# A token-mixing transformer block on one core: another order of scores, projections and sums in the last cycle of attention, from score tile 998 on

## The chip, the core and the metric

The kernel runs on one core of one Trainium2 chip. Its time is the device time of one launch in microseconds (us); the time of a version is the median of a few runs. The engines named here are PE (TensorE, with PEld for its weight loads), ACT (ScalarE), DVE (VectorE), POOL (GpSimd) and SP, which issues the DMAs. Each engine works through its own queue in order and waits on semaphores for the others.

## What is computed

Two layers, each of them multi-query attention (32 query heads, one key and value head) and a token-mixing MLP, over a sequence of 2048 tokens of width 512. Both parts start with a layer norm and add to the residual. Cut to what matters:

```python
def _A_ref(x, wq, wk, wv, wo):            # S = 2048, D = 512, H = 32, Dh = 16
    q = (x @ wq).reshape(B, S, H, Dh).transpose(0, 2, 1, 3)
    k = x @ wk
    v = x @ wv
    scores = jnp.einsum("bhqd,bkd->bhqk", q, k) * (Dh ** -0.5)
    p = softmax(scores, axis=-1)
    o = jnp.einsum("bhqk,bkd->bhqd", p, v)
    return o.transpose(0, 2, 1, 3).reshape(B, S, H * Dh) @ wo

def _B_ref(x, w1, b1, w2, b2):            # F = 1792
    h = _layernorm(x)
    u = gelu(jnp.einsum("bsd,sf->bdf", h, w1) + b1)
    y = jnp.einsum("bdf,fs->bds", u, w2) + b2
    return y.transpose(0, 2, 1)

for _ in range(2):
    x = x + _A_ref(_layernorm(x), A_wq, A_wk, A_wv, A_wo)
    x = x + _B_ref(_layernorm(x), B_w1, B_b1, B_w2, B_b2)
```

## The kernel before

**Attention in tiles.** A layer's attention is cut into 32 groups: group i has four heads and one block of 512 queries. A group has 32 score tiles: 16 key tiles of 128 keys (kt) times two pairs of heads (j0 = 0 or 2). So a layer has 1024 tiles, and tile 998 is group 31 (the last), kt = 3, j0 = 0. A tile's name below is sc_31_3_0, its exponentials are p_31_3_0, and its sums go into acc_31. Tile 998 is reached once in each layer.

A tile passes three steps:

- `scores` (line 921): two matmuls of 51 rows put the scores of two heads into a PSUM pair `sc`. There are three such pairs (`bufs=3`), so a score waits until the tile three before it has left its pair.
- line 931: ACT takes the exponential from the pair into an SBUF tile `p`. For a **copied** tile DVE first copies the pair to SBUF (line 929), which frees the pair, and ACT works on the copy in place.
- `sums` (line 937): matmuls of 32 columns add p times the values (and a column of ones, the softmax's denominator) into `acc`.

There are 12 buffers for p: eight of one pool (`NP`) and, from the third guard on, every third tile uses one of four others (`NMORE`).

**Other work between the tiles.** When two groups (eight heads) are done, DVE divides by the denominators (lines 857 to 863) and writes `hl`. A projection (line 898) multiplies 128 tokens of it by a part of `wo` into a PSUM bank `po`; DVE adds the bank to the residual `x` (line 906). The projections of one turn use the same bank, so one waits for the addition of the one before. At tile 998 four projections po_14_0 to po_14_3 of one part, three matmuls each, are due. The MLP's own products (line 1214) run after attention has ended, in `rest`, beginning with pu_e.

**What sets the order.** `Attention.run` writes every engine's queue by hand, by tuples of numbers ("turns"). A number from 1 to 9 stands for that many scores; 11 to 19 for as many as its last digit, the last of them copied; 0 for the next of the other parts (here a projection); -n for the sums of the n oldest tiles that wait. At each negative number there is also a slot in which small DVE work may be put (`mix.step`). `Mixer.turn` chooses the tuple: FOURS is taken where four projections are due, 30 tiles of the last group are still to be summed, and more than 992 tiles are scored. It is taken at tile 998, once in each layer. The turns behind it are PLAIN, two scores and then as many sums as leave two tiles waiting:

```python
PLAIN = (2, -2)
...
if len(self.projections) > 3 and att.to_boundary() == 30 and att.scored > 2 * NKT * (NB * NG - 1):
    return FOURS, [projection] * 4
```

Of the kernel before, what the change touches and what calls it, by code (L numbers as in the profile page):

```python
# [45 lines left out]
    2, -2, 13, 0, 13, -4, 13, 0, 13, -4, 3, -6, 13, 0, 13, 0, 3, -6, 13, -4, 3, -4,  # L46
)
ENTRY = (1, 0, 13, 0, 13, -4, 13, -4, 13, -4, 13, -4)
FOURS = (3, -4, 12, 0, 13, 0, -4, 3, -4, 12, 0, 13, -4, 0)
SHORT = (2, 0, 3, -4, 3, -4)  # L50
TINY = (2, 0, 2, -4)
PLAIN = (2, -2)
# [20 lines left out]
def kernel(  # L73
# [729 lines left out]
    class Attention:  # L803
# [193 lines left out]
        def run(self, mix, proj):  # L997
# [10 lines left out]
            while self.scored < total:  # L1008
# [31 lines left out]
                for k in turn:  # L1040
# [15 lines left out]
                    else:  # L1056
# [11 lines left out]
                        if self.pieces:  # L1068
                            self.pieces.pop(0)()
                        elif turn in (LONG, COPIED, ENTRY, DOUBLE, QUAD, QUAD_TO_FOUR, FOURS, WHOLE):  # L1070
                            room = 2.4 if turn in (COPIED, ENTRY, QUAD, QUAD_TO_FOUR) else 1.0
# [15 lines left out]
    class Mixer:  # L1087
# [150 lines left out]
        def turn(self, att):  # L1238
# [20 lines left out]
            if len(self.projections) > 3 and att.to_boundary() == 30 and att.scored > 2 * NKT * (NB * NG - 1):  # L1259
                return FOURS, [projection] * 4  # L1260
            if len(self.projections) > 1:
# [473 lines left out]
```

## Time and profile before

| | us |
|---|---|
| runs (3), median | 2511.52 |
| runs, lowest to highest | 2510.51 to 2512.19 |
| the profiled execution: its own time | 2511.45 |
| the profiled execution: span from first to last instruction | 2509.7 |
| busy in the span: PE, ACT, DVE, POOL | 2493.1, 2102.5, 1554.8, 148.2 |
| FOURS and the turns behind it, layer 0: first score, first product behind attention | 1013.14, 1041.00 |

A timeline's row has a start, a duration (both us), the engine, the line, the operation with what it writes and reads, and how many instructions are merged in it; in brackets stands the idle time before it and what ended that. A score tile is two matmuls, so "sc x6" is three tiles; the sums of a tile are four, so "acc x16" are the sums of four tiles. PE's durations overlap those behind them, so what a piece costs on PE is the distance from its start to the next piece's start.

### The profile page before, as it was taken

How to read it: one execution, taken by the hardware profiler on the slowest of the kernel's cores; microseconds unless marked ns; L12 is line 12 of the kernel's file. 1: busy time of each engine (PE TensorE's matmuls, PEld its weight loads, DVE VectorE, ACT ScalarE, POOL GpSimd, SP SyncE). 2: the span in 40 equal slices, each digit the busy share in tenths (PEclk: the TensorE clock that was granted, in tenths of full speed). 3: DMA queues.
4: the chain of work that ended last, by engine and by line, in shares of the span. 5: the costliest groups of instructions: out<-in, count | busy, mean ns of one | idle time of the engine just before them, and what ended most of it. 6: DMA issues, size and time to landing. Idle time of an engine off the chain costs nothing. (4 is left out here: it accounts for less than half of the span.)

```text
span 2509.7 us, 41974 instructions
## 1 busy us (share of the span) xinstructions
PE 2493.1 (99%) x16170; PEld 1242.5 (50%) x16170; DVE 1554.8 (62%) x2462; ACT 2102.5 (84%) x2345; POOL 148.2 (6%) x235
## 2 busy tenths in 40 slices
PE   9999999999999999999999999999999999999999
PEld 6444344444444444588864343444444444445887
DVE  6565566667766776564445565666677667765522
ACT  6999999999999999653349999999999999995511
POOL 5000000000000000141000000000000000002200
PEclk9999999999999999999999999999999999999999
DMA  3221201111111111134414112111111111102343
GB/s 116 75 66 41 65 29 39 32 41 31 39 31 39 31 41 31 43 110 149 127 51 126 51 47 57 31 39 31 41 31 39 31 43 33 41 26 67 106 125 95
DMA packets 168679, 143.56 MB, mean 57 GB/s; under 512 B 17650, under 2 KB 132368, under 8 KB 167952
## 3 DMA queue, kind: packets, MB, share of 16 engines
q1 hardware_dynamic: 168464, 140.72, 18.9%
q8 instruction: 132, 2.16, 0.4%
q14 instruction: 83, 0.68, 0.1%
HBM read 97.67 MB, written 26.22 MB: 49 GB/s over the span
## 5 line engine op out<-in xcount | busy, mean ns | idle before, releaser
L931 ACT ACTIVATE p<-sc 128x1024 f32<-128x1024 f32 x1441 | 1404.4, 1050 | 63.5 <-PE sc L921 62.7
L929 DVE COPY p<-sc 128x1024 f32<-128x1024 f32 x607 | 742.7, 1224 | 525.2 <-PE sc L921 439.6
L937 PE MATMUL acc<-p,vaug 128*32 128x512 f32 x8192 | 999.7, 600 | 0.0
L921 PE MATMUL sc<-qs,kst 51*128 51x512 f32 x4096 | 683.4, 432 | 8.2 <-DVE kst L595 2.7
L931 ACT ACTIVATE p<-p 128x1024 f32<-128x1024 f32 x607 | 659.4, 1086 | 12.9 <-DVE p L929 8.2
L921 PEld LDWEIGHTS sc<-qs,kst 51*128 51x128 f32 x4096 | 338.8, 185 | 560.1 <-ACT p L931 390.2
L937 PEld LDWEIGHTS acc<-p,vaug 128*32 128x32 f32 x8192 | 218.6, 109 | 488.9 <-issue 474.6
L1467 PE MATMUL py<-u,w 128*128 128x512 f32 x1344 | 307.4, 390 | 0.0
L1467 PEld LDWEIGHTS py<-u,w 128*128 128x128 f32 x1344 | 251.9, 188 | 52.3
L1455 ACT CAST w<-w2r 128x896 fp32r<-128x896 f32 x64 | 60.3, 945 | 185.6 <-PE py L1467 177.8
L1214 PE MATMUL pu<-hb,w 128*128 128x512 f32 x792 | 209.6, 406 | 0.0
L1214 PEld LDWEIGHTS pu<-hb,w 128*128 128x128 f32 x792 | 140.9, 188 | 57.7 <-issue 31.8
L1201 POOL TENSOR_TENSOR w<-w1r,w 128x256 fp32r<-128x256 f32 x86 | 69.9, 821 | 1572.9 <-ACT w L1199 1571.8
L1456 DVE TENSOR_TENSOR w<-w2r,w 128x896 fp32r<-128x896 f32 x64 | 72.3, 1130 | 110.7 <-ACT w L1455 110.7
L857 DVE RECIPROCAL o<-o 128x128 f32<-128x128 f32 x120 | 113.3, 944 | 8.8 <-DMA o<-ev 8.8
L898 PE MATMUL po<-wo,hl 128*128 128x512 f32 x360 | 100.5, 412 | 0.1
L418 PE MATMUL pq<-hT,wq 128*128 128x512 f32 x312 | 81.4, 404 | 0.0
L898 PEld LDWEIGHTS po<-wo,hl 128*128 128x128 f32 x360 | 62.6, 188 | 34.0 <-issue 16.4
L839 DVE COPY ev<-acc 128x512 f32<-128x512 f32 x64 | 43.6, 682 | 56.0 <-PE acc L937 56.0
L1214 PE MATMUL pu_l<-hb,w 128*128 128x512 f32 x336 | 77.1, 389 | 0.0
L1473 DVE SCALAR_TENSOR_TENSOR x<-py,b2c,x 128x512 f32<-128x512 f32 x32 | 24.0, 750 | 81.6 <-PE py L1467 81.6
L1199 ACT CAST w<-w1r 128x256 fp32r<-128x256 f32 x86 | 34.3, 406 | 47.3 <-PE pu_l L1214 12.7
(191 smaller groups left out, 1181.9 us busy)
## 6 DMA issues: line engine op xcount, KB each, us to landing
w1r<-in_B_w_dram SPq DMA_DIRECT2D x224, 128.0 KB
w2r<-in_B_w_dram SPq DMA_DIRECT2D x64, 448.0 KB
qs<-qd SPq DMA_DIRECT2D x384, 64.0 KB
qd<-q SPq DMA_DIRECT2D x64, 256.0 KB
o<-ev SPq DMA_DIRECT2D x128, 128.0 KB
x<-in_A_x_dram SPq DMA_DIRECT2D x16, 256.0 KB
hd<-hT SPq DMA_DIRECT2D x2, 2048.0 KB
out_dram<-x SPq DMA_DIRECT2D x16, 256.0 KB
```

What stands on the lines that cost most here:

```text
L418: yield nc.tensor.matmul(out, a, c, start=(k == 0), stop=(k == len(terms) - 1))
L857: nc.vector.reciprocal(o[:, 1, c], o[:, 1, c])
L898: nc.tensor.matmul(po, a, c, start=(k == 0), stop=(k == 3 * len(parts) - 1))
L921: nc.tensor.matmul(sc[:, j, :], kst[kt // 4][rows, kt % 4 * P : (kt % 4 + 1) * P], qs[i % NQ][rows, j0 // 2, :], start=True, stop=True,)
L929: nc.vector.tensor_copy(pt, sc)
L931: nc.scalar.activation(pt, sc, AF.Exp, scale=0.25)
L937: nc.tensor.matmul(self.acc[i][c : c + 32, :], vaug[:, kt].rearrange("p d k -> p (d k)"), pt[:, j, :], start=(kt == 0), stop=(kt == NKT - ...
L1201: eng.tensor_tensor(w[:, 1], raw, f32(w[:, 0]), op=ALU.subtract)
L1214: nc.tensor.matmul(pu, a, c, start=(start and k == 0), stop=(stop and k == 5))
L1455: nc.scalar.copy(w[:, 0], raw)
L1456: nc.vector.tensor_tensor(w[:, 1], raw, f32(w[:, 0]), op=ALU.subtract)
L1467: nc.tensor.matmul(py, a, d, start=(c == 0 and f == 0 and k == 0), stop=(c == 1 and f == NFH - 1 and k == 2),)
```

## The change

One tuple has other numbers. Both have 16 scores, 16 sums, four projections and four slots; one more score is copied by DVE in the new one.

```diff
 ENTRY = (1, 0, 13, 0, 13, -4, 13, -4, 13, -4, 13, -4)
-FOURS = (3, -4, 12, 0, 13, 0, -4, 3, -4, 12, 0, 13, -4, 0)
+FOURS = (-2, 13, 0, 13, 0, 13, 0, -2, -6, 13, 0, 13, -6, 1)
 SHORT = (2, 0, 3, -4, 3, -4)
```

PE's queue at tile 998 of layer 0, before:

```order
L921 MATMUL sc_31_3_0_10975<-qs_90,kst_84 128x512 x2
L921 MATMUL sc_31_3_2_10980<-qs_90,kst_84 128x512 x2
L921 MATMUL sc_31_4_0_10985<-qs_90,kst_85 128x512 x2
L937 MATMUL acc_31_10967<-p_31_1_0_10925,vaug 32x512 x2
L937 MATMUL acc_31_10967<-p_31_1_2_10945,vaug 32x512 x2
L937 MATMUL acc_31_10967<-p_31_2_0_10950,vaug 32x512 x2
L937 MATMUL acc_31_10967<-p_31_2_2_10955,vaug 32x512 x2
L921 MATMUL sc_31_4_2_10998<-qs_90,kst_85 128x512 x2
L921 MATMUL sc_31_5_0_11003<-qs_90,kst_85 128x512 x2
L898 MATMUL po_14_0_11009<-wo_1151,hl_14_10757 128x512 x3
L921 MATMUL sc_31_5_2_11014<-qs_90,kst_85 128x512 x2
```

The same place with the change:

```order
L937 MATMUL acc_31_10967<-p_31_1_0_10925,vaug 32x512 x2
L937 MATMUL acc_31_10967<-p_31_1_2_10945,vaug 32x512 x2
L921 MATMUL sc_31_3_0_10979<-qs_90,kst_84 128x512 x2
L921 MATMUL sc_31_3_2_10984<-qs_90,kst_84 128x512 x2
L921 MATMUL sc_31_4_0_10989<-qs_90,kst_85 128x512 x2
L898 MATMUL po_14_0_10995<-wo_1151,hl_14_10757 128x512 x3
L921 MATMUL sc_31_4_2_11000<-qs_90,kst_85 128x512 x2
L921 MATMUL sc_31_5_0_11005<-qs_90,kst_85 128x512 x2
L921 MATMUL sc_31_5_2_11010<-qs_90,kst_85 128x512 x2
L898 MATMUL po_14_1_11016<-wo_1151,hl_14_10757 128x512 x3
```

Two tiles' sums stand ahead of tile 998 now, and blocks of three scores and a projection follow each other without sums between them; a third such block (6_0, 6_2, 7_0 and po_14_2) follows.

PE's queue behind that third block, before (where po_14_2 stands later, behind 9_0):

```order
L921 MATMUL sc_31_7_0_11043<-qs_90,kst_85 128x512 x2
L921 MATMUL sc_31_7_2_11048<-qs_90,kst_85 128x512 x2
L921 MATMUL sc_31_8_0_11053<-qs_90,kst_86 128x512 x2
L937 MATMUL acc_31_10967<-p_31_5_0_11006,vaug 32x512 x2
L937 MATMUL acc_31_10967<-p_31_5_2_11017,vaug 32x512 x2
L937 MATMUL acc_31_10967<-p_31_6_0_11022,vaug 32x512 x2
L937 MATMUL acc_31_10967<-p_31_6_2_11027,vaug 32x512 x2
L921 MATMUL sc_31_8_2_11066<-qs_90,kst_86 128x512 x2
```

And with the change:

```order
L921 MATMUL sc_31_7_0_11031<-qs_90,kst_85 128x512 x2
L898 MATMUL po_14_2_11037<-wo_1151,hl_14_10757 128x512 x3
L937 MATMUL acc_31_10967<-p_31_2_0_10950,vaug 32x512 x2
L937 MATMUL acc_31_10967<-p_31_2_2_10955,vaug 32x512 x2
L937 MATMUL acc_31_10967<-p_31_3_0_10982,vaug 32x512 x2
L937 MATMUL acc_31_10967<-p_31_3_2_10987,vaug 32x512 x2
L937 MATMUL acc_31_10967<-p_31_4_0_10992,vaug 32x512 x2
L937 MATMUL acc_31_10967<-p_31_4_2_11003,vaug 32x512 x2
L937 MATMUL acc_31_10967<-p_31_5_0_11008,vaug 32x512 x2
L937 MATMUL acc_31_10967<-p_31_5_2_11013,vaug 32x512 x2
L921 MATMUL sc_31_7_2_11058<-qs_90,kst_85 128x512 x2
```

Eight tiles' sums stand in one run between the scores of 7_0 and 7_2, where four stood between blocks of three before. Further on, 8_0, 8_2, po_14_3, 9_0, 9_2 and 10_0 follow, then six sums in one run, then 10_2 and the PLAIN turns as before: 11_0, 11_2, the sums of 9_0 to 10_2, and 12_0.

DVE's queue in the same stretch, with the change:

```order
L863 TENSOR_TENSOR hl_14_10757<-o_28_10380,hl_14_10757 128x128
L929 COPY p_31_4_0_10992<-sc_31_4_0_10989 128x1024
L906 TENSOR_TENSOR x_80<-x_80,po_14_0_10995 128x512
L929 COPY p_31_5_2_11013<-sc_31_5_2_11010 128x1024
L906 TENSOR_TENSOR x_81<-x_81,po_14_1_11016 128x512
L929 COPY p_31_7_0_11034<-sc_31_7_0_11031 128x1024
L906 TENSOR_TENSOR x_82<-x_82,po_14_2_11037 128x512
L929 COPY p_31_8_2_11071<-sc_31_8_2_11068 128x1024
L906 TENSOR_TENSOR x_83<-x_83,po_14_3_11074 128x512
L929 COPY p_31_10_0_11092<-sc_31_10_0_11089 128x1024
```

Before, the copies stood at 5_0, 6_2, 9_0 and 10_2, each ahead of one of the four additions, and there was no fifth. The queues of POOL and SP keep their order. Layer 1 is changed in the same way.

## The prediction, on record before the changed kernel was run

> **What bounds the kernel now.** I read the page first, then the chain of waits, then ACT and PE row by row around the first of the two places that change.
>
> ```profile
> PE 2493.1 (99%) x16170; PEld 1242.5 (50%) x16170; DVE 1554.8 (62%) x2462; ACT 2102.5 (84%) x2345; POOL 148.2 (6%) x235
> ```
>
> By this line PE is never idle, but a PE row also contains the time in which a matmul that has been issued waits for data. So I look at the chain that ended last, at the end of layer 1's attention (start, length, what):
>
> ```profile
> 2276.47 1.85 PE acc L937 x16
> 2278.33 0.67 PE sc L921 x4
> 2278.99 1.00 PE acc L937 x8
> 2279.99 0.66 PE sc L921 x4
> 2280.65 1.26 PE acc L937 x8
> ...
> 2284.40 3.00 PE acc L937 x16
> 2287.40 2.99 PE pu_e L1214 x12
> ```
>
> The same four tiles' sums cost 1.85 us at the top and 3.00 at the bottom. The difference is waiting for exponentials, and it ends in the first product of the MLP. So what delays ACT's last exponential delays all that follows. ACT's rows in layer 0, from tile 3_0 (at 1013.97) on, those at which its spacing changes:
>
> ```profile
> 1013.97 1.04 ACT L931 ACTIVATE p<-sc 128x1024 f32<-128x1024 f32 x1
> 1016.68 1.07 ACT L931 ACTIVATE p<-sc 128x1024 f32<-128x1024 f32 x1
> 1017.99 1.06 ACT L931 ACTIVATE p<-p 128x1024 f32<-128x1024 f32 x1 [0.23 <-DVE p L929]
> 1018.95 1.01 ACT L931 ACTIVATE p<-sc 128x1024 f32<-128x1024 f32 x1
> 1020.76 1.06 ACT L931 ACTIVATE p<-p 128x1024 f32<-128x1024 f32 x1
> 1021.95 1.02 ACT L931 ACTIVATE p<-sc 128x1024 f32<-128x1024 f32 x1
> 1024.70 1.03 ACT L931 ACTIVATE p<-sc 128x1024 f32<-128x1024 f32 x1
> 1026.20 1.06 ACT L931 ACTIVATE p<-p 128x1024 f32<-128x1024 f32 x1 [0.47 <-DVE p L929]
> 1030.94 1.01 ACT L931 ACTIVATE p<-sc 128x1024 f32<-128x1024 f32 x1
> 1032.53 1.02 ACT L931 ACTIVATE p<-sc 128x1024 f32<-128x1024 f32 x1 [0.58 <-PE sc L921]
> 1038.88 1.09 ACT L931 ACTIVATE p<-sc 128x1024 f32<-128x1024 f32 x1
> ```
>
> Unhindered, an exponential from PSUM takes 0.905 from start to start (1013.97 to 1016.68 is three of them), and a copied one 0.955 (1017.99 to 1018.95). From 12_0 (1032.53) to 15_2 (1038.88), seven steps take 6.35, so there ACT is the bound and whatever moves 12_0 moves the end by as much. From 3_0 to 12_0 there are 18 steps in 18.56 us; 14 x 0.905 + 4 x 0.955 is 16.49, so ACT **starves for 2.07 us** per layer. That is the quantity on which the change acts. PE's rows beside it, with the prices of its pieces (start to next start):
>
> ```profile
> 974.37 2.78 PE L937 MATMUL acc<-p,vaug 128*32 128x512 f32 x24
> 977.08 0.97 PE L921 MATMUL sc<-qs,kst 51*128 51x512 f32 x6
> ...
> 1013.14 0.96 PE L921 MATMUL sc<-qs,kst 51*128 51x512 f32 x6
> 1013.48 0.62 PE L921 MATMUL sc<-qs,kst 51*128 51x512 f32 x4
> 1014.03 1.92 PE L937 MATMUL acc<-p,vaug 128*32 128x512 f32 x16
> 1015.88 0.73 PE L921 MATMUL sc<-qs,kst 51*128 51x512 f32 x4
> 1016.55 0.97 PE L898 MATMUL po<-wo,hl 128*128 128x512 f32 x3
> 1017.45 1.10 PE L921 MATMUL sc<-qs,kst 51*128 51x512 f32 x6
> ...
> 1021.35 0.97 PE L921 MATMUL sc<-qs,kst 51*128 51x512 f32 x6
> 1031.93 0.73 PE L921 MATMUL sc<-qs,kst 51*128 51x512 f32 x4
> 1032.59 1.07 PE L937 MATMUL acc<-p,vaug 128*32 128x512 f32 x8
> 1033.59 0.73 PE L921 MATMUL sc<-qs,kst 51*128 51x512 f32 x4
> ```
>
> Three scores cost 0.89, of which 0.55 from the second's start; two cost 0.67; a projection costs 0.90. Sums cost 1.00 for two tiles, 1.85 for four, 2.71 for six, so 0.86 for each pair more. Three scores take 0.89 on PE and 2.72 to 2.77 on ACT, so PE fills the three PSUM pairs and then waits for ACT, as it does once already:
>
> ```profile
> 1017.81 0.38 PEld L921 LDWEIGHTS sc<-qs,kst 51*128 51x128 f32 x4 [0.18 <-ACT p L931]
> ```
>
> This is the weight load of 6_0, held until the exponential of 4_2 (the 1016.68 row), three tiles before, had left its pair: 1.13 after that began; in a row of exponentials they last 1.02, so I take **1.10** (between 1.07 and 1.13). And a starved ACT begins **0.60** after the score's start: 1021.35 to 1021.95, and 1031.93 to 1032.53.
>
> **The change, step by step, in one layer.** PE reaches the stretch at 1013.14, ACT is free for 3_0 at 1013.97. Nothing ahead of it has moved. I follow where ACT starves in the new order.
>
> *The two tiles' sums first.* 1013.14 + 1.00 for the sums + 0.60 is 1014.74, when 3_0 can begin: ACT waits **0.77** where it waited for nothing.
>
> *The three projections three tiles apart.* Here ACT is fed from full pairs and sets the pace. Let E be the start of 5_0's exponential. 6_2 takes over 5_0's pair at E + 1.10; from there 7_0 and its handing over cost 0.55, po_14_2 0.90, and the run of eight sums 3.57 (2.71 + 0.86, an estimate from the rows, since no run of eight is shown here). So 7_2's score begins at E + 6.12 and can be taken up at E + 6.72. Meanwhile ACT has 5_0, 5_2 (copied), 6_0, 6_2 and 7_0 (copied): 3 x 0.905 + 2 x 0.955 = 4.63. ACT waits **2.09**.
>
> *The six sums.* With E the start of 8_0's: 9_2 at E + 1.10, then 0.55, six sums 2.71 and 0.60 make E + 4.96, against the same 4.63. ACT waits **0.33**.
>
> *The end.* From 10_2's score, three scores (0.89) and four sums (1.85) make 2.74 until 12_0's, against three exponentials, 2.72: **0.02**.
>
> Together 3.21 instead of 2.07, and one more copied tile costs ACT 0.05: **1.19 us per layer**, twice **2.4 us**. From 12_0 on the queues are the old ones and ACT is the bound as before, so nothing of it is given back.
>
> What is covered: DVE's work per block is one copy and one addition.
>
> ```profile
> 1013.78 0.29 DVE L863 TENSOR_TENSOR hl<-o,hl 128x128 fp32r<-128x128 f32 x1
> 1016.73 1.22 DVE L929 COPY p<-sc 128x1024 f32<-128x1024 f32 x1 [2.65 <-PE sc L921]
> 1017.87 0.68 DVE L906 TENSOR_TENSOR x<-x,po 128x512 f32<-128x512 f32 x1
> ```
>
> That is 1.14 + 0.68 = 1.82 us in a block of 2.77 on ACT, so the fifth copy, and the wait of one projection for the addition of the one before, lie beside ACT's work. The cover is 0.95 per block; beyond it each microsecond on DVE would delay the block by as much. `hl` is ready at 1014.07, and the first projection comes after the sums and three scores, 1013.14 + 1.00 + 0.89 = 1015.03. Up to eleven tiles wait for their sums (from 2_0 to 7_0); there are 12 buffers, and 7_0 takes that of 1_0, summed at the start, so no buffer is waited for. No DMA is issued in the stretch on either side, the division of tile 14's part is done, and the four slots find nothing to place, so SP, POOL and the rest of DVE are not touched.
>
> The second place is the same; its rows stand 16.64 apart as here 1015.88 and 1032.53 do (16.65):
>
> ```profile
> 2262.22 0.73 PE L921 MATMUL sc<-qs,kst 51*128 51x512 f32 x4
> 2278.86 7.44 ACT L931 ACTIVATE p<-sc 128x1024 f32<-128x1024 f32 x8 [0.58 <-PE sc L921]
> ```
>
> The profiled execution took 2511.45 (span 2509.7) and the median is 2511.52, 0.07 apart, so the sum is put on the median: **2513.9**. The bounds: 3.44 to 3.70 for the eight sums (eight at the 0.43 of a pair's half; twice 1.85), 1.07 to 1.13 for a pair's release twice. They leave 1.0 to 1.4 per layer; with the runs' own spread of 0.8 to each side the case lies between 2512.7 and 2515.1.
>
> **The rivals.** *PE's work alone counts.* The page's 99% and a chain that is PE nearly throughout speak for it. Until 12_0's score PE had blocks of 3, 2, 3, 3, 2, 3 and 2 scores, 4 x 0.89 + 3 x 0.67 = 5.57, and five runs of sums, 9.25; now it has six blocks of three, 5.34, and runs of 2, 8, 6 and 4, 1.00 + 3.57 + 2.71 + 1.85 = 9.13. That is 0.35 less per layer, so 2510.8. It decides if the pairs come free early enough that no score waits. Against it: the 1017.81 row waits already after a single block, and the stretch took 18.79 for 18.42 of work; the forecast needs 1.9 us of waiting in it. Chance 0.12. The Trainium skill's page "TensorEngine Tiling (Array Packing)", Key Properties, says that changing the tiling mode drains TensorE; scores, sums and projections use three shapes, and the new order changes shape less often, so by that rule the change ends at this rival's time. The rows above agree that a change of shape costs something (two sums 1.00, but 0.86 for two more).
>
> *The clock drops, and it ends slower.* In the blocks of projections PE waits for some 0.4 to 0.6 us before several scores, some 1.3 us in three. If that lowered the granted clock to half for the run of eight sums, they would cost 3.57 more per layer: 2513.9 + 7.1 = 2521.0. It decides from the point where waiting of this density is punished. Against it stands the end of attention, where the sums wait likewise:
>
> ```profile
> 1034.20:1041.00 6.80, 6.80 (x42) 1.75 (x40) 0.00 (x0) 6.05 (x8) 0.67 (x1) 1.00 0.00 0
> ```
>
> The granted clock there (third from the end) is 1.00. Chance 0.04. The Trainium skill's page "TensorE: Matmul & The Clock Gate", section "A second HAM failure mode: psum-queue depth-cycling", says that small idle pieces at PSUM's hand-over can make the clock swing between half and full; that rule would give this rival's time, and the row just shown disagrees with it so far.
>
> *ACT no longer starves.* More tiles are scored ahead, and if those covered the long runs of sums, 2.07 per layer would go: 2507.4. It decides if more than 3.57 + 0.90 + 0.60 us of exponentials were ready as PE turns to the eight sums. But a score needs a pair, and only a copied tile waits outside, so there are at most three. Chance 0.03. *The branch isn't taken* and nothing changes, 2511.5: both engines' queues show the new order, so 0.01.
>
> **How the numbers follow.** The forecast has 0.80, the rivals 0.12, 0.04, 0.03 and 0.01. The range takes in the first rival and the forecast's bounds, with some tenths beyond each for what a launch varies: 2510.6 to 2515.8. A measurement of this kernel tells about 0.2% (5 us) from no change. The forecast (0.1%) and the first, third and last rival lie within; slower by more are the clock and a forecast mis-sized by a factor of two, 0.06; faster by more is nearly excluded, since even an ACT that never starves gains 0.16%: 0.02.
>
> **What would show it.** In the changed profile, ACT should wait about 0.8 before 3_0, 2.1 before 7_2 and 0.3 before 10_2, and not between 4_0 and 7_0; weight loads of scores should wait for ACT in the first three blocks; from 12_0 to pu_e all should be as long as before, and pu_e begin 1.2 later at layer 0 and 2.4 at layer 1. I am wrong if 7_2's exponential follows 7_0's closely (more tiles were ready than I count), if a projection waits for DVE's addition after PE's other waits are over, or if the granted clock falls below 1.00 in the stretch.

## The result, and the profile after

| | before | with the change |
|---|---|---|
| runs, median (22 each), us | 2512.10 | 2515.47 |
| runs, lowest to highest, us | 2509.75 to 2513.86 | 2513.13 to 2517.85 |
| span of the profiled execution, us | 2509.7 | 2512.0 |

The ratio is 1.0013, with a 95% interval from 1.0007 to 1.0019: the change costs 3.4 us, between 1.8 and 4.8. The time moved the way that was forecast. It lies in the range, above the forecast of 2513.9 by 1.6; of these, 0.6 come from the base, whose median was 2511.52 over three runs and is 2512.10 over 22. The prediction had said that a measurement of this kernel tells about 0.2% from no change; 22 runs of each kernel told 0.13%. One of the 15 runs of the kernel before that were taken beside the experiments needed 8570.69 us at a mean granted clock of 0.265, and the interval given below leaves it out.

The page's totals hardly move, and that is the first thing to see: the line that said nothing before says nothing now.

```profile
PE 2492.3 (99%) x16170; PEld 1242.6 (49%) x16170; DVE 1556.4 (62%) x2464; ACT 2102.4 (84%) x2345; POOL 147.9 (6%) x235
```

The change shows in ACT's timeline in layer 0 (start, duration, operation, number merged, idle time and what ended it), from the tile ahead of 998 on:

```profile
1012.08 1.08 ACT L931 ACTIVATE p<-p 128x1024 f32<-128x1024 f32 x1
1013.66 1.94 ACT L931 ACTIVATE p<-sc 128x1024 f32<-128x1024 f32 x2 [0.51 <-PE sc L921]
1015.48 1.06 ACT L931 ACTIVATE p<-p 128x1024 f32<-128x1024 f32 x1
1016.43 1.94 ACT L931 ACTIVATE p<-sc 128x1024 f32<-128x1024 f32 x2
1018.24 1.08 ACT L931 ACTIVATE p<-p 128x1024 f32<-128x1024 f32 x1
1019.19 1.96 ACT L931 ACTIVATE p<-sc 128x1024 f32<-128x1024 f32 x2
1021.00 1.09 ACT L931 ACTIVATE p<-p 128x1024 f32<-128x1024 f32 x1
1024.15 1.94 ACT L931 ACTIVATE p<-sc 128x1024 f32<-128x1024 f32 x2 [2.07 <-PE sc L921]
1025.98 1.06 ACT L931 ACTIVATE p<-p 128x1024 f32<-128x1024 f32 x1
1026.93 1.94 ACT L931 ACTIVATE p<-sc 128x1024 f32<-128x1024 f32 x2
1028.74 1.08 ACT L931 ACTIVATE p<-p 128x1024 f32<-128x1024 f32 x1
1030.13 10.19 ACT L931 ACTIVATE p<-sc 128x1024 f32<-128x1024 f32 x11 [0.32 <-PE sc L921]
```

The first row is 2_2, then come 3_0 (1013.66), 7_2 (1024.15) and 10_2 (1030.13). Before each of these three ACT is idle and PE's scores end the wait; from 3_0 to 7_0 and from 7_2 to 10_0 it is fed without a gap, and the last eleven run in one piece. Counted from start to start, with 0.905 or 0.955 for the tile ahead, it waits 0.62, 2.19 and 0.43 there. PE's timeline shows the other side:

```profile
1010.34 2.78 PE L937 MATMUL acc<-p,vaug 128*32 128x512 f32 x24
1013.06 0.97 PE L921 MATMUL sc<-qs,kst 51*128 51x512 f32 x6
1013.95 0.96 PE L898 MATMUL po<-wo,hl 128*128 128x512 f32 x3
1014.85 0.51 PE L921 MATMUL sc<-qs,kst 51*128 51x512 f32 x2
1015.65 0.73 PE L921 MATMUL sc<-qs,kst 51*128 51x512 f32 x4 [0.30 <-ACT p L931]
1016.31 0.97 PE L898 MATMUL po<-wo,hl 128*128 128x512 f32 x3
1017.51 0.50 PE L921 MATMUL sc<-qs,kst 51*128 51x512 f32 x2 [0.23 <-ACT p L931]
1018.42 0.73 PE L921 MATMUL sc<-qs,kst 51*128 51x512 f32 x4 [0.41 <-ACT p L931]
1019.09 0.96 PE L898 MATMUL po<-wo,hl 128*128 128x512 f32 x3
1019.98 3.64 PE L937 MATMUL acc<-p,vaug 128*32 128x512 f32 x32
1023.55 0.96 PE L921 MATMUL sc<-qs,kst 51*128 51x512 f32 x6
...
1041.36 3.06 PE L1214 MATMUL pu_e<-hb,w 128*128 128x512 f32 x12
```

The first row is four tiles' sums of the turn ahead and the two that the change puts first, in one run. In the blocks with projections PE waits for ACT to empty PSUM pairs; then it turns to eight tiles' sums (1019.98 to 1023.55) and ACT, with the rest of 6_0 and two more tiles left, runs dry. Each engine waits for the other in turn.

To compare executions I measure **the stretch**: from the start of 2_2's exponential, the tile ahead of 998, to the start of pu_e. Before it is 1013.02 to 1041.00 in layer 0, 27.98 us, and 27.98 in layer 1 (2259.35 to 2287.33). With the change it is 29.28 (1012.08 to 1041.36) and 29.46 (2260.11 to 2289.57): 1.30 and 1.48 more, together 2.8 us.

The spans differ by 2.3 only, because something else moved: the stretch of layer 0 begins 0.94 earlier. The windows' rows (length, busy times, and third from the end the granted clock) show why, before and then with the change:

```profile
45.00:55.00 10.00, 8.81 (x51) 3.28 (x49) 6.01 (x17) 7.98 (x9) 1.04 (x1) 0.83 0.35 95
```

```profile
45.00:55.00 10.00, 8.81 (x60) 3.78 (x63) 5.92 (x17) 8.96 (x10) 1.04 (x1) 1.00 0.37 96
```

At the entry to layer 0, 960 us ahead of the change, the clock fell in the one execution and not in the other. That belongs to the execution and not to the kernel: two more executions of the changed kernel, below, had 0.66 and 0.83 there. From pu_e of layer 1 to the end the kernel before and the three traces of the changed kernel take 222.4 to 222.5 alike. So a span says less than the stretch.

### The profile page after: what moved, and what is told of

It is laid out like the page before. It is cut to its first block, busy times and chain, and to the rows that moved or that the text cites. A ratio compares the mean times of both kernels' runs of the same rounds, so it can differ in the third digit from the quotient of the medians.

```text
span 2512.0 us, 41976 instructions
## 1 busy us (share of the span) xinstructions
PE 2492.3 (99%) x16170; PEld 1242.6 (49%) x16170; DVE 1556.4 (62%) x2464; ACT 2102.4 (84%) x2345; POOL 147.9 (6%) x235
```

## The experiments

All change only the tuple FOURS of the kernel before; the changed kernel has `(-2, 13, 0, 13, 0, 13, 0, -2, -6, 13, 0, 13, -6, 1)`. My theory was that ACT starves while PE works through long runs of sums. The rivals were that only PE's work counts, that the projections or the fifth copy cost the time, and that the clock falls.

### The sums first, alone

```diff
-FOURS = (3, -4, 12, 0, 13, 0, -4, 3, -4, 12, 0, 13, -4, 0)
+FOURS = (-2, 3, -2, 12, 0, 13, 0, -4, 3, -4, 12, 0, 13, -4, 0)
```

> The old order with only its first run of four sums parted: two tiles' sums ahead of tile 998, two behind its three scores. Measured by the stretch from the exponential of 2_2 (the tile ahead of 998) to the start of pu_e: 27.98 us before, 29.28 with the whole change in layer 0. Theory (ACT starves while PE sums, and starving at the start is not made up): ACT waits about 0.6 before 3_0 and the stretch is 28.5, 0.5 longer than before. Rival (only PE's work counts): 0.86 + 1.00 in place of 1.85 for the sums, so 28.0.

The stretch is 28.44 in both layers (1015.03 to 1043.47; 2262.45 to 2290.89), 0.46 longer than before. ACT's timeline:

```profile
1015.03 1.07 ACT L931 ACTIVATE p<-p 128x1024 f32<-128x1024 f32 x1
1016.60 3.77 ACT L931 ACTIVATE p<-sc 128x1024 f32<-128x1024 f32 x4 [0.50 <-PE sc L921]
1020.46 1.06 ACT L931 ACTIVATE p<-p 128x1024 f32<-128x1024 f32 x1
```

The wait before 3_0 is there, 0.62 from start to start, and PE's work, the same within 0.01, doesn't predict it. A part is made up at once: 5_0 waits 0.24 here and waited 0.40 before, and 0.62 less these 0.16 are the 0.46. So two sums moved ahead cost alone about a third of the whole loss.

### The eight sums parted

```diff
-FOURS = (-2, 13, 0, 13, 0, 13, 0, -2, -6, 13, 0, 13, -6, 1)
+FOURS = (-2, 13, 0, 13, 0, -4, 13, 0, -4, 13, 0, 13, -6, 1)
```

> The changed order with its run of eight sums parted: four between the second and the third block of three scores, four behind the third. Projections, copies and the six sums as in the change. Theory: the one wait of 2.2 us before 7_2 becomes about 0.5 before 6_0 and 0.9 before 7_2, and the stretch is 28.6, between before (27.98) and the change (29.28). Rival (the loss comes from PE's waits for PSUM pairs between the projections, or from the fifth copy on DVE, and not from the long run of sums): it stays at 29.1 to 29.3, or the waits before 6_0 and 7_2 together are still 2.2.

The stretch is 28.42 in layer 0 (1012.23 to 1040.65) and 28.59 in layer 1 (2259.45 to 2288.04), 0.86 and 0.87 shorter than with the change. The copies, the projections and the six sums are those of the change. ACT's two rows at the places named:

```profile
1019.83 1.94 ACT L931 ACTIVATE p<-sc 128x1024 f32<-128x1024 f32 x2 [0.35 <-PE sc L921]
1021.65 1.06 ACT L931 ACTIVATE p<-p 128x1024 f32<-128x1024 f32 x1
1023.47 1.94 ACT L931 ACTIVATE p<-sc 128x1024 f32<-128x1024 f32 x2 [0.76 <-PE sc L921]
```

One wait of 2.07 in the profile's count has become 0.35 and 0.76, together 1.11; counted from start to start as above, 2.19 has become 0.48 and 0.87, which are the 0.85 that the stretch shows. So the run of eight costs 0.86 of the 1.30 per layer, and the projections and the fifth copy, which stayed, don't explain that part. PE's own waits before 6_0 and 6_2 (0.23 and 0.41 with the change) went with it, so the run doesn't tell eight sums in one run from sums that come late.

### No copies

```diff
-FOURS = (-2, 13, 0, 13, 0, 13, 0, -2, -6, 13, 0, 13, -6, 1)
+FOURS = (-2, 3, 0, 3, 0, 3, 0, -2, -6, 3, 0, 3, -6, 1)
```

> The changed order with none of its five scores copied by DVE, so all are read by ACT out of PSUM. PE's work is the same and ACT's is 0.25 less. Theory (what ACT still has when PE turns to the long runs of sums is what the three pairs and one copied tile hold; without the copy it is one tile less): ACT waits about 3.0 before 7_2 and 1.2 before 10_2, and the stretch is 30.6, 1.3 longer than with the change. Rival (the copies cost time, or are not part of it): 29.0 to 29.3.

Layer 0 does what was expected: 30.61 (1015.50 to 1046.11). The second and third of ACT's rows begin with 7_2 and 10_2:

```profile
1017.08 8.36 ACT L931 ACTIVATE p<-sc 128x1024 f32<-128x1024 f32 x9 [0.50 <-PE sc L921]
1028.24 5.61 ACT L931 ACTIVATE p<-sc 128x1024 f32<-128x1024 f32 x6 [2.80 <-PE sc L921]
1034.88 10.19 ACT L931 ACTIVATE p<-sc 128x1024 f32<-128x1024 f32 x11 [1.04 <-PE sc L921]
```

Nine exponentials at 0.905 from 1017.08 end at 1025.22, so ACT waits 3.0 there, and 1.2 before the third row. It has less to do and starves longer. The copied tile is not a cost but a store: it gives its PSUM pair back early, and so one tile more is ready when PE turns to the sums. The rival on the copies falls.

Layer 1 was not expected: 33.23 (2264.45 to 2297.68). PE's timeline and the windows of that run:

```profile
1024.06 3.64 PE L937 MATMUL acc<-p,vaug 128*32 128x512 f32 x32
...
2270.27 2.20 PE L921 MATMUL sc<-qs,kst 51*128 51x512 f32 x6
2272.41 1.65 PE L898 MATMUL po<-wo,hl 128*128 128x512 f32 x3
2273.98 5.29 PE L937 MATMUL acc<-p,vaug 128*32 128x512 f32 x32
```

```profile
2272.00:2280.00 8.00, 8.00 (x43) 2.47 (x41) 0.69 (x1) 2.58 (x4) 0.00 (x0) 0.67 0.00 0
1024.00:1029.00 5.00, 5.00 (x41) 1.85 (x41) 0.69 (x1) 2.20 (x3) 0.00 (x0) 1.00 0.00 0
```

The same eight sums take 3.64 at a clock of 1.00 and 5.29 where it was 0.67 in the window. The stretch is 2.6 longer than that of layer 0, less than the 3.57 that the prediction's second rival charged per layer. So a fallen clock is seen here, in a kernel where PE waits more than in the change; that the waits set it off isn't shown. Three more executions were to tell whether it also acts in the change.

### The change twice more, and no copies once more

> The changed kernel once more, for another execution's trace. Theory (the loss is ACT's starving, the same in each execution): the stretch from the exponential of 2_2 to pu_e is 29.2 to 29.5 in both layers, with 2.2 us of waiting before 7_2, and the granted clock in both is 1.00. Rival (the clock drops there in some executions, as it did in layer 1 without the copies, which would explain why the median rose by more than the two stretches): a stretch above 31 in one layer of this run or the next, at a granted clock below 0.9.

> The changed kernel a third time, with the same expectations: theory 29.2 to 29.5 in both layers at a granted clock of 1.00, rival above 31 in a layer at a clock below 0.9.

> The changed order without copies once more (its first run gave 30.61 in layer 0 at a granted clock of 1.00, and 33.23 in layer 1, where the clock was 0.67 in 8 us). Theory (PE's waiting between the scores is near what lowers the clock, and whether it does depends on where the execution stands): 30.6 where the clock stays, about 33 where it falls, and not the same layers as before is possible. Rival (something fixed in layer 1, not the clock): 30.6 and 33.2 again in the same layers, with no drop of the clock.

| stretch, us | layer 0 | layer 1 |
|---|---|---|
| change, first | 29.28 | 29.46 |
| change, second | 29.26 | 29.43 |
| change, third | 29.28 | 29.47 |
| no copies, first | 30.61 | 33.23 |
| no copies, second | 30.60 | 30.60 |

The windows' rows of the first execution, layer 0 and then layer 1:

```profile
1013.00:1042.25 29.25, 28.01 (x184) 10.30 (x181) 9.33 (x11) 24.72 (x28) 0.72 (x1) 1.00 0.03 10
2260.00:2290.00 30.00, 28.76 (x190) 10.08 (x183) 9.91 (x14) 25.86 (x29) 0.73 (x1) 1.00 0.03 10
```

In all six stretches of the change the clock was 1.00, and those of one layer agree within 0.04. Without copies, one stretch of four lost its clock, and the other three agree within 0.01. So the drop is no part of layer 1's code; whether it comes depends on the execution. For the change it isn't seen; that it never comes, six stretches don't show.

### An order that beats both

```diff
-FOURS = (3, -4, 12, 0, 13, 0, -4, 3, -4, 12, 0, 13, -4, 0)
+FOURS = (13, -4, 13, -2, 0, 13, -2, 0, 13, 0, -2, 13, -4, 13, -4, 13, -2, 0, 3, -4, 2, -4)
```

> An order for the 26 scores from tile 998 to the end of attention in which no block of PE is much longer than the 2.77 us that ACT takes for three tiles: three scores (the last copied) and four sums, or three scores, two sums and a projection; the sums that this leaves over, and the fourth projection, come in the last turns, where PE waits for ACT in the old order. The same work but two copies more than with the change. Theory: ACT waits nowhere for more than 0.2, the stretch is 26.4, 1.6 shorter than before per layer, and the time 3.2 us (0.13%) below before. Rival (PE had 18.42 us of work in the 18.79 up to 12_0, so no order gains more than the rest): 27.6 or more, and no difference in time.

The stretch is 26.10 and 26.11 (1012.26 to 1038.36; 2255.40 to 2281.51), 1.88 and 1.87 shorter than before, 0.3 per layer better than expected. In time it is 2507.02 (11 runs) against 2510.88 for the kernel before on the same chip: a ratio of 0.9984, interval 0.9975 to 0.9993, so 3.9 us faster, between 1.8 and 6.3; the stretches say 3.75. The 2.07 that ACT waited before, less 0.15 for three more copied tiles, are 1.92, so nearly all of the waiting is gone. How much of that the even blocks bring, and how much the copies, this run doesn't tell apart. ACT's timeline has no gap marked from 2_2 on; its last rows and pu_e:

```profile
1028.79 1.19 ACT L931 ACTIVATE p<-p 128x1024 f32<-128x1024 f32 x1
1029.74 2.07 ACT L931 ACTIVATE p<-sc 128x1024 f32<-128x1024 f32 x2
1031.55 1.21 ACT L931 ACTIVATE p<-p 128x1024 f32<-128x1024 f32 x1
1032.50 4.83 ACT L931 ACTIVATE p<-sc 128x1024 f32<-128x1024 f32 x5
```

```profile
1034.51 0.74 PE L921 MATMUL sc<-qs,kst 51*128 51x512 f32 x4
1035.17 3.26 PE L937 MATMUL acc<-p,vaug 128*32 128x512 f32 x24
1038.36 3.01 PE L1214 MATMUL pu_e<-hb,w 128*128 128x512 f32 x12
```

The exponentials are still 0.905 and 0.955 apart, but each is listed as longer (1.19 and 1.21 for a copied one, 1.06 where ACT has just waited). So the spacing, not the listed length, is what one costs.

## Why the prediction was right

**What bounds.** Right. From 12_0 to the end ACT was the bound in both kernels, and nothing that was lost before was given back; in layer 1 a little more was lost there (below).

**The terms.** Each of the waits came where it was put, and their sum was 3.3 (with 0.05 in the last eleven) for a forecast 3.21; before it was 2.07. That the sum came so close is in part luck: one wait was 0.15 shorter and two were 0.10 longer each.

- Before 3_0: 0.62 for 0.77. I charged the two sums 1.00, the price of a run of two. But four sums stand right ahead of them, so they prolong a run and cost the 0.86 of one more pair. The queue ahead of the change was not to be left out here.
- Before 7_2: 2.19 for 2.09. The run of eight, an estimate, cost exactly its 3.57 (1019.98 to 1023.55), and the starved start its 0.60 (1023.55 to 1024.15). The 0.10 lies in 6_2 and 7_0: a score that has waited begins a new block, and the two cost 0.67 (1018.42 to 1019.09) where I charged 0.55.
- Before 10_2: 0.43 for 0.33, for the same reason (1026.15 to 1026.81 in the change's trace).
- The fifth copy's 0.05 is too small to be seen apart. That DVE's work was covered shows in the projections, of which the second and third began when PE was ready (1016.31 and 1019.09, 0.66 and 0.67 behind two scores), and in the run without copies, which was slower.

Layer 0 so lost 1.30 for a forecast 1.19. **Layer 1** lost 1.48: one exponential of the last eleven, that of 13_0, began some 0.18 late there, in all three traces of the change. ACT's rows for the eleven in the first two:

```profile
2278.16 10.38 ACT L931 ACTIVATE p<-sc 128x1024 f32<-128x1024 f32 x11 [0.32 <-PE sc L921]
2279.83 10.37 ACT L931 ACTIVATE p<-sc 128x1024 f32<-128x1024 f32 x11 [0.32 <-PE sc L921]
```

In layer 0 they take 10.19. The run with the eight sums parted has 10.38 in layer 1 too, and the runs without copies have 10.19. The prediction expected nothing of it, and its cause stays open.

**The sum.** 2.8 us in the two stretches for a forecast 2.4; 3.4 between the medians, whose interval takes in both numbers. The measured 2515.47 lies above 2515.1, the top of the forecast's own bounds, and in the range by the tenths that it added; the base that had moved and layer 1's 0.18 have a part in that. Whether the 0.6 between stretches and medians is real stays open.

**The rivals.** PE's work alone (2510.8) fell with the result, which is 4.7 above it, and with the sums-first run: the same work, 0.46 more per layer. That ACT no longer starves (2507.4) fell for the change, for the reason given there, three tiles ready at most; the even order reaches that time, with shorter blocks between the scores and a copied tile in nearly every one. The clock didn't fall in the change's six stretches. That it can fall within such a stretch the run without copies shows. The Trainium skill's page "TensorE: Matmul & The Clock Gate", section "A second HAM failure mode: psum-queue depth-cycling", describes small waits at PSUM's hand-over and a clock that swings. That trace agrees as far as one fall goes, 0.67 over 8 us, and shows no swinging; the change's traces, with waits of 0.23 to 0.41 on the same engine, stayed at 1.00 (from start to start these three waits are 0.46, 0.30 and 0.57, the 1.3 that the prediction gave).

## What to carry to other kernels

Where two engines feed each other through a few buffers, compare each block that the one works through with what the other has ready at that moment, and not the sums of their work: the same matmuls were 1.3 us slower per layer where one block of three scores, a projection and eight tiles' sums held 5.36 us of PE's work (0.89 + 0.90 + 3.57) against the 2.77 of three tiles on ACT, and 1.9 faster with blocks of about 2.75 each and three more copies. Work that the consumer doesn't need at once (here sums and projections) belongs where the producer waits anyway, in the last turns; the even order shows this together with its other changes, not alone. And an engine that reads as 99% busy can be the one that waits: look for the gaps of its partner.

## What I had not expected

- The granted clock falls at the entry to layer 0 in some executions and not in others (at the entry to layer 1, 1290 to 1310 us, it was 0.83 or 0.91 in all nine traces): 1.00, 0.83, 0.66 and 0.83 from 45 to 55 us in four executions, the first, third and fourth of them of the changed kernel. Executions of one kernel differ by as much as 2.8 us before the change's first place is reached (2_2 begins at 1012.08 in one execution of the changed kernel and at 1014.87 in another), as much as the whole effect. In all nine traces, whose code is the same up to there, the start goes with that clock: 1012.08 to 1012.26 at 1.00 (three traces), 1013.02 and 1013.50 at 0.83, and 1014.66 to 1015.50 at 0.66 or 0.67 (four). Only a stretch with fixed ends shows 1 us in a single trace of such a kernel.
- One stretch without copies had PE at a lower clock through its run of eight sums, 5.29 us for 3.64, after waits of 0.3 to 0.4 before nearly every score.
